# Loads re-placed, head gates from a 0/1 table, swapped K halves and a last store from ScalarE, in a fused attention and feed-forward kernel

## The chip, the cores and the metric

The kernel runs on one core of one Trainium2 chip. The metric is device time in microseconds (us) of one execution; lower is better. The engines are named PE (TensorE, with its weight loads as PEld), DVE (VectorE), ACT (ScalarE), POOL (GpSimd) and SP (SyncE, which here only issues transfers).

## What is computed

One input x of 2048 tokens by 512 columns, bf16, goes through two branches that are mixed by a gate per token. Attention runs in four segments of 512 tokens with 32 heads of 16 columns; later segments also read a memory that the earlier ones wrote.

```python
def _A_ref(x, wq, wk, wv, wo, beta):            # H = 32, N = 4 segments, L = 512
    q, k, v = ...                               # x @ wq, x @ wk, x @ wv by head and segment
    phi = lambda t: jnp.where(t > 0, t + 1.0, jnp.exp(t))
    g = _sigmoid(beta).reshape(1, H, 1, 1)
    for s in range(N):
        logits = qs @ ks^T * scale + causal mask
        a_dot = softmax(logits) @ vs
        a_mem = (phi(qs) @ M) / (phi(qs) @ z + 1e-06)
        outs.append(g * a_mem + (1.0 - g) * a_dot)
        M = M + phi(ks)^T @ vs
        z = z + phi(ks) summed over tokens
    return concat(outs) @ wo

def _B_ref(x, W_gate, W_up, W_down):            # 512 -> 1792 -> 512
    return (relu(x @ W_gate) * (x @ W_up)) @ W_down

g = _sigmoid((x * gate_w).sum(-1, keepdims=True))
return g * _A_ref(x, ...) + (1 - g) * _B_ref(x, ...)
```

## The kernel before

All work is a list of tasks. Each task has an engine and a function that writes its instructions, and the table ORDER says in which order the tasks are written out. Each engine works through its own instructions in that order, and waits on semaphores for what other engines and transfers have to deliver. A second table, UNITS, says which PSUM bank or ring buffer each result takes.

**Segments and units.** The work on a segment is cut into four units of eight heads. A unit has four scores (`qk`, L626), each 8 matmuls on 32 rows into four PSUM banks, followed by one exponential on ACT (L648) into a buffer E. A mask on POOL (L677) sets what lies above the diagonal to zero. Every second unit has a fifth score for the diagonal blocks (`qk_diag`, L639, with L659 as its mask on DVE). The product with V (`pv`, L699) is two sets of 32 matmuls on 32 columns each, one for even heads (r = 0) and one for odd heads (r = 1); it reads V from `Vp`, and for the diagonal blocks from `Vm`, a copy by `fill_vm` (L612) that has the first half of each key block twice.

**Between the scores.** The projections, the feed-forward matmuls and the output matmuls fill PE's time between the scores. They are written by `full` either as one matmul on the whole array (L469) or as four on a quarter of the columns each (L473), whichever fits the tile shape in use.

**K.** `proj_k` casts k from PSUM into `ktr` (L575) and then multiplies it by 0/1 columns (L578): `mcol_e` keeps the rows of even heads, `mcol_o` those of odd heads. A key block is 128 keys, held as two halves of 64. `KT` has five halves for each block: two of even heads, one extra first half of even heads, and two of odd heads. The diagonal score reads the two that stand in the middle, first halves of even and of odd heads. That makes three products for each unit.

**Head gates.** `head_gates` works on 32 gates (L386 to L388). `row_gates` then copies, for each quarter of the partitions, the gates that this quarter needs (L393, L395, five copies for each of four quarters), and `pair_gates` finishes (L399).

**Loads.** All loads are issued at the start, on SP's queue, but for three on ACT's (L266): half of the first x quarter (`xn`), wq row block 1, and wq row blocks 2 and 3 in one transfer. The second half of the first segment's x comes transposed by the transfer (`xT`, L304); the first half is transposed by PE. The weights of the down projection (`wd`) and of the output projection (`wo`, L325 and L327) are the last of these loads. On SP's queue everything later, such as transposes of `pkT` (L591), the next segment's x (L276), the coefficients (L773, L787) and the output stores (L900), comes behind them.

**The end.** The last output tile is computed in columns 0 to 255, then 256 to 383 and 384 to 511. DVE scales each part by the token's gate (L895), and SP issues two stores (L900).

Of the kernel before, what the change touches and what calls it, by code (L numbers as in the profile page):

```python
# [12 lines left out]
P = 128  # L13
# [165 lines left out]
def kernel(  # L179
# [74 lines left out]
    def work():  # L254
        return plan.one("ps", range(7, -1, -1))


    LANDS = dict(n0=3470, n1=3600, q0=4650, q1=4650, x0=6300, qb=6000, ka=7900, kb=9300,
                 v=11500, g0=13000, u0=14000, gw=14800, be=15100, g1=16300, u1=17500, n2=18500,
                 x1=21500, g2=22800, u2=23900, g3=25000, u3=26100, d0=28900, d1=31600, o=34400)  # L260

    def arrival(name):
# [717 lines left out]
```

## Time and profile before

| | |
|---|---|
| three runs | 264.25 us (median), 263.18 to 264.29 |
| the profiled execution | 264.48 us, of which its span is 262.7 |
| PE busy | 257.8 us, 98% of the span |
| DVE, ACT, POOL busy | 204.9 us (78%), 183.7 us (70%), 64.2 us (24%) |
| granted TensorE clock | 1.0 |
| transfers | 19.72 MB, mean 75 GB/s |

Matmuls are pipelined and their ends are modelled, so a busy PE is not PE at its peak. The other engines count only for what PE has to wait for. In rows of the timeline the columns are start, length, engine, line, operation, result and operands, count, and in square brackets the idle time in front with what ended it. In rows of groups they are busy time and mean duration in ns of one, then the idle time in front of them. In tables by stage the columns are the stretch, its length, busy time and count for each engine, granted clock, share of the DMA engines, and GB/s.

### The profile page before, as it was taken

What the parts mean: (1) busy time and instruction counts of PE and PEld (TensorE: products, weight loads), DVE (VectorE), ACT (ScalarE), POOL (GpSimd) and SP (SyncE); (2) the same over time, 40 slices, a digit from 0 to 9 for tenths busy, and PEclk for the clock granted to TensorE, in tenths of its full rate; (3) what the DMA queues carried; (4) which work ended last, traced back from release to release, by engine and by line L of the source; (5) the groups of instructions that cost most, each with busy time, mean ns of one, the idle gap of its engine ahead of it and who ended that gap; (6) DMA issues with size and microseconds to landing.
All of it is one profiled execution on the core that took longest, in us unless ns stands there. A gap on an engine that the chain in (4) does not pass through costs nothing.

```text
span 262.7 us, 8841 instructions
## 1 busy us (share of the span) xinstructions
PE 257.8 (98%) x3828; PEld 117.4 (45%) x3828; DVE 204.9 (78%) x472; ACT 183.7 (70%) x168; POOL 64.2 (24%) x168
## 2 busy tenths in 40 slices
PE   8899999999999999999999999999999999999995
PEld 3344434454444454444444445444444444444454
DVE  2798999999995756959989789676998858688722
ACT  3199889999788678888486776878568759873000
POOL 8022732212321423232031223133121243121000
PEclk9999999999999999999999999999999999999999
DMA  6999984110711201200220111320110200311011
GB/s 146 337 304 323 273 192 53 22 24 10 116 25 52 92 22 39 76 2 2 80 41 4 56 20 36 110 85 2 24 57 3 56 2 22 102 30 73 2 42 42
DMA packets 31566, 19.72 MB, mean 75 GB/s; under 512 B 16040, under 2 KB 29992, under 8 KB 31528
## 3 DMA queue, kind: packets, MB, share of 16 engines
q1 hardware_dynamic: 30840, 18.64, 26.2%
q8 instruction: 30, 0.49, 0.9%
q10 hardware_dynamic: 688, 0.52, 0.9%
q14 instruction: 8, 0.07, 0.1%
HBM read 13.21 MB, written 2.55 MB: 60 GB/s over the span
## 4 chain that ended last, share of the span: by engine, by line
PE 94%; DMA 2%; DVE 2%; SPq 0%; issue 0%
PE ps L469 56%; PE ps L473 20%; PE ps L626 8%; PE ps L699 7%; DMA xT<-in_A_x_dram 2%; PE ps L639 1%; DVE QT L559 1%; PE ps L819 1%; PE ps L795 0%; PE ps L755 0%; SPq L266 0%; DVE KT L578 0%; DVE ktr L575 0%; DVE osr L895 0%
## 5 line engine op out<-in xcount | busy, mean ns | idle before, releaser
L648 ACT ACTIVATE E<-ps 128x2048 bf16<-128x2048 f32 x64 | 120.2, 1877 | 27.3 <-PE ps L626 18.8
L677 POOL TENSOR_SCALAR_AFFINE_SELECT E<-E 128x256 bf16<-128x256 bf16 x128 | 54.8, 452 | 169.8 <-ACT E L648 169.8
L869 DVE TENSOR_TENSOR hT<-ps,rgr 128x512 bf16<-128x512 f32 x56 | 38.0, 684 | 17.0 <-PE ps L469 12.6
L469 PE MATMUL ps<-xT,wu_sb 128*128 128x512 bf16 x168 | 45.9, 380 | 0.0
L469 PE MATMUL ps<-xT,wg_sb 128*128 128x512 bf16 x154 | 42.0, 380 | 0.0
L863 ACT ACTIVATE rgr<-ps 128x512 bf16<-128x512 f32 x56 | 32.5, 599 | 13.4 <-PE ps L473 6.9
L469 PE MATMUL ps<-wd_sb,hT 128*128 128x512 bf16 (+1 forms) x174 | 40.3, 354 | 0.0
L730 DVE STREAM_TRANSPOSE T<-ps 128x512 f32<-128x512 f32 x32 | 22.2, 707 | 7.8 <-PE ps L699 7.7
L626 PE MATMUL ps<-QT,KT 32*128 32x320 bf16 (+3 forms) x512 | 25.4, 273 | 0.1
L469 PEld LDWEIGHTS <-wu_sb 128*128 128x128 bf16 x168 | 15.1, 98 | 18.7 <-issue 2.7
L469 PEld LDWEIGHTS <-hT 128*128 128x128 bf16 x174 | 15.2, 98 | 17.1 <-issue 2.1
L469 PEld LDWEIGHTS <-wg_sb 128*128 128x128 bf16 x154 | 14.4, 98 | 17.7 <-issue 1.3
L895 DVE TENSOR_SCALAR osr<-ps,ngcol 128x512 bf16<-128x512 f32 (+2 forms) x18 | 12.2, 685 | 11.2 <-PE ps L473 5.7
L699 PE MATMUL ps<-E,Vp 128*17 128x320 bf16 (+3 forms) x512 | 19.3, 274 | 0.0
L626 PEld LDWEIGHTS <-KT 32*128 32x128 bf16 x512 | 7.6, 92 | 25.5 <-issue 24.2
L473 PE MATMUL ps<-xT,wg_sb 128*32 128x512 bf16 x280 | 18.6, 379 | 0.0
L648 ACT ACTIVATE Em<-ps 128x2048 bf16<-128x2048 f32 x8 | 15.0, 1876 | 5.0 <-PE ps L639 5.0
L473 PE MATMUL ps<-wd_sb,hT 128*32 128x512 bf16 (+1 forms) x312 | 17.8, 360 | 0.0
L469 PE MATMUL ps<-xT,wq_sb 128*128 128x512 bf16 x60 | 16.4, 382 | 1.0 <-DMA xT<-in_A_x_dram 1.0
L469 PE MATMUL ps<-wv_sb,xT 128*128 128x512 bf16 x62 | 16.9, 380 | 0.0
L559 DVE CAST QT<-ps 128x512 bf16<-128x512 f32 x16 | 10.7, 687 | 6.4 <-PE ps L469 6.2
L473 PE MATMUL ps<-xT,wu_sb 128*32 128x512 bf16 x224 | 15.1, 379 | 0.0
(102 smaller groups left out, 301.3 us busy)
## 6 DMA issues: line engine op xcount, KB each, us to landing
out_dram<-osr SPq DMA_DIRECT2D x15, 128.0 KB
wd_sb<-in_B_W_down_dram SPq DMA_DIRECT2D x2, 896.0 KB
xn<-in_A_x_dram SPq DMA_DIRECT2D x3, 512.0 KB
cdr<-coefs SPq DMA_DIRECT2D x6, 256.0 KB
xn<-coefs SPq DMA_DIRECT2D x6, 256.0 KB
wg_sb<-in_B_W_gate_dram SPq DMA_DIRECT2D x2, 512.0 KB
wu_sb<-in_B_W_up_dram SPq DMA_DIRECT2D x2, 512.0 KB
wg_sb<-in_B_W_gate_dram SPq DMA_DIRECT2D x2, 384.0 KB
```

The lines of the kernel that those rows point to most:

```text
L469: nc.tensor.matmul(out, lhsT=lhsT, rhs=rhs, start=start, stop=stop)
L473: nc.tensor.matmul(out[r], lhsT=lhsT[:, r], rhs=rhs, start=start, stop=stop, tile_position=(0, 32 * j))
L559: prj["q", seg, c] = plan.add("DVE", 600, key - RQK, lambda: nc.vector.tensor_copy(QT[i][:], bank(sl)), [a], DVL, frees=[sl])
L626: nc.tensor.matmul(ps[:, j * L + o:j * L + o + L - q], lhsT=KT[i][rows, kb, 3 * r:3 * r + 2].rearrange("p h q -> p (h q)"), rhs=QT[i][rows ...
L639: nc.tensor.matmul(ps[:, o:o + HP], lhsT=KT[i][rows, kb, 2:4].rearrange("p h q -> p (h q)"), rhs=QT[i][rows, kb * P:kb * P + HP], start=Tr ...
L648: last_exp[0] = [plan.add("ACT", 66 + 4 * L / 1.2, key, lambda: nc.scalar.activation(dst, ps[:, 0:4 * L], ACT.Exp, scale=SCALE), [a] + war ...
L677: nc.gpsimd.affine_select(out=m[:, :, o:o + HP], in_=m[:, :, o:o + HP], compare_op=ALU.is_ge, fill=0.0, base=HP, pattern=[[0, 4], [1, HP]] ...
L699: nc.tensor.matmul(bank(sl)[32 * m:32 * m + HW, q:q + w], lhsT=(Vp[i] if n < 4 else Vm)[:, kb, r, 4 * c + j, 0:HW], rhs=rhs, start=(n == 0 ...
L730: done.append(plan.add("DVE", 633, key - RL, lambda r=r, sl=sl: nc.vector.transpose(T[ts.i][:, r], bank(sl)), [a] + done, 75 if r else 0, ...
L863: r = plan.add("ACT", 478, key - RL, lambda sl=gsl, rs=rs: nc.scalar.activation(rgr[rs.i][:], bank(sl), ACT.Relu), [g], ACL, frees=[gsl])
L869: nc.vector.tensor_tensor(hT[hs1.i][:], bank(sl), rgr[rs.i][:], ALU.mult)),
L895: nc.vector.tensor_scalar(osr[os.i][:, n0 - c0:n1 - c0], bank(sl)[:, 0:n1 - n0], ngcol[:, tt:tt + 1], None, ALU.mult)),
```

## The change

1. **Loads.** wq row blocks 2 and 3 become two transfers on SP's queue, issued behind the transposing load of x, in place of one on ACT's. The q matmuls of the first segment wait for each row block. `wd` and `wo` become tasks of their own (`load_late`) that ORDER places later on SP's queue, among the first segment's transfers.
2. **Head gates.** POOL fills a 0/1 table `pick` by memsets. DVE multiplies it with beta and sums over four columns, which leaves in each partition the betas it needs; then one exponential and five small DVE operations follow.
3. **K halves.** `KT` has four halves: even heads second half first, then odd heads in the usual order. The middle two are again the first halves, so the third product is gone. Since the even heads' keys are swapped within each block, so must be V: `Vs` is a copy of the even heads' V with halves swapped, made by two transfers for each segment on SP's queue. `pv` for even heads waits for it. POOL masks only half of the partitions for even heads.
4. **The end.** ACT scales the last 128 columns, and ACT's queue issues the last store.
5. **Order.** ORDER and UNITS are replaced whole (not shown). Among other things six v matmuls now stand ahead of the first score.

```diff
+    Vs = sb([P, 4, H // 2, 18], BF16, "Vs")
-    KT = [sb([P, 4, 5, P // 2], BF16, f"KT{i}") for i in range(RQ)]
+    KT = [sb([P, 4, 4, P // 2], BF16, f"KT{i}") for i in range(RQ)]
...
-    got_q = [load(eng, wq_sb[:, ci, :], A_wq[ci * P:(ci + 1) * P, :], "q%d" % ci)
-             for ci, eng in enumerate((nc.sync, nc.scalar))]
+    def load_wq(eng, ci):
+        return load(eng, wq_sb[:, ci, :], A_wq[ci * P:(ci + 1) * P, :], "q%d" % ci)
+    got_q = [load_wq(nc.sync, 0), load_wq(nc.scalar, 1)]
     nc.sync.dma_start_transpose(out=xT[0][:, NC // 2:NC, :], in_=x[0:L, halves[1]])
-    got_q.append(load_rows(nc.scalar, wq_sb, A_wq, 1, "q"))
+    got_q += [load_wq(nc.sync, ci) for ci in range(2, NC)]
...
-    got_d = [load_wd(0, 7, "d0"), load_wd(7, NF, "d1")]
-    (seven wo transfers at the start)
+    def load_late():
+        for j, (f0, f1) in enumerate(((0, 7), (7, NF))):
+            got_d.append(plan.add("SP", 1270, K(2 + j), lambda f0=f0, f1=f1: nc.sync.dma_start(
+                out=wd_sb[:, f0:f1, :], ...
+        for c in range(NC):
+            ...
+            got_o.append(plan.add("SP", 1250 if c else 600, K(4, c), wo, lat=3500, xfer=450.0))
...
+    nc.gpsimd.memset(pick[:], 0.0)
+    for m in range(4):
+        rows = slice(32 * m, 32 * m + 32)
+        nc.gpsimd.memset(pick[rows, 1, :, m], 1.0)
+        for c in range(NC):
+            nc.gpsimd.memset(pick[rows, 0, c, (m + c) % 4], 1.0)
+    def pick_heads():
+        nc.vector.tensor_tensor(gsel..., pick..., betab[:, None, :].to_broadcast([P, 2, H]), ALU.mult)
+        nc.vector.tensor_reduce(out=gcat..., in_=gsel..., axis=mybir.AxisListType.X, op=ALU.add)
...
-                KT[u % RQ][:, :, o:o + w],
-                ktr[ks.i].rearrange("p (k h q) -> p k h q", k=4, h=2)[:, :, 0:w], m[:, 0:1],
+                KT[u % RQ][:, :, 2 * n:2 * n + 2],
+                ktr[ks.i].rearrange("p (k h q) -> p k h q", k=4, h=2)[:, :, ::1 if n else -1],
+                m[:, 0:1],
...
+        att["vs", seg] = [plan.add("SP", 600, K(4 * seg - 2 - (1 if seg else 0), 2000), lambda h=h: (
+            nc.sync.dma_start(out=Vs[64 - 64 * h:128 - 64 * h], in_=Vp[i][64 * h:64 * h + 64, :, 0])),
+            ... for h in range(2)]
...
+                half = slice(0, P) if r else slice(0, HP)
                 for _, _, o in PIECES[k]:
-                    nc.gpsimd.affine_select(out=m[:, :, o:o + HP], in_=m[:, :, o:o + HP],
+                    nc.gpsimd.affine_select(out=m[half, :, o:o + HP], in_=m[half, :, o:o + HP],
...
-                            lhsT=(Vp[i] if n < 4 else Vm)[:, kb, r, 4 * c + j, 0:HW],
+                            lhsT=(Vm[:, kb, r] if n > 3 else Vp[i][:, kb, 1] if r else
+                                  Vs[:, kb])[:, 4 * c + j, 0:HW],
...
+            last = w == P and n1 == D
+                if last:
+                    nc.scalar.activation(dst, src, ACT.Copy, scale=g)
+                else:
+                    nc.vector.tensor_scalar(dst, src, g, None, ALU.mult)
+        queue = nc.scalar if last else nc.sync
```

More of the change, by code (lines that the diff above doesn't have):

```diff
@@ L390, in row_gates @@
-    def row_gates(m):
-        g = gall.rearrange("p k (c j r) -> p k c j r", j=4, r=2)
-        rows = slice(32 * m, 32 * m + 32)
-        nc.vector.tensor_copy(gcat[rows, 1], g[rows, 1, :, m])
-        for c in range(NC):
-            nc.vector.tensor_copy(gcat[rows, 0, c], g[rows, 0, c, (m + c) % 4])
-    def pair_gates():
-        for r, m in enumerate((mcol_e, mcol_o)):
-            nc.vector.tensor_scalar(bdg[:, :, r], gcat[:, 1, :, r], m[:, 0:1], None, ALU.mult)
-    got_eb = plan.add("ACT", 200, 0.0, lambda: nc.scalar.activation(
-        eb[:], betab[:], ACT.Exp, scale=-1.0), [got_be], 100)
@@ L403 @@
-    got_gates = plan.add("DVE", 700, 0.0, head_gates, [got_eb], 100, lock=True)
-    got_gates = [plan.add("DVE", 560, 0.0, lambda m=m: row_gates(m), [got_gates], 100, lock=True)
-                 for m in range(4)]
-    got_gates = plan.add("DVE", 300, 0.0, pair_gates, got_gates, 100, lock=True)
+    def pick_heads():
+        nc.vector.tensor_tensor(
+            gsel.rearrange("p k c j r -> p k (c j r)"), pick.rearrange("p k c j r -> p k (c j r)"),
+            betab[:, None, :].to_broadcast([P, 2, H]), ALU.mult)
+        nc.vector.tensor_reduce(out=gcat.rearrange("p k c r -> p (k c) r"),
+                                in_=gsel.rearrange("p k c j r -> p (k c) r j"),
+                                axis=mybir.AxisListType.X, op=ALU.add)
@@ new lines, in head_gates @@
+    def head_gates():
+        nc.vector.tensor_scalar(rcat[:], gcat[:], 1.0, None, ALU.add)
+        nc.vector.reciprocal(rcat[:], rcat[:])
+        nc.vector.tensor_tensor(gcat[:, 0], gcat[:, 0], rcat[:, 0], ALU.mult)
+        for r, m in enumerate((mcol_e, mcol_o)):
+            nc.vector.tensor_scalar(bdg[:, :, r], rcat[:, 1, :, r], m[:, 0:1], None, ALU.mult)
+    got_gates = plan.add("DVE", 380, 0.0, pick_heads, [got_be], 100, lock=True)
+    got_gates = plan.add("ACT", 200, 0.0, lambda: nc.scalar.activation(
+        gcat[:], gcat[:], ACT.Exp, scale=-1.0), [got_gates], 100)
@@ L408 @@
+    got_gates = plan.add("DVE", 850, 0.0, head_gates, [got_gates], 100, lock=True)
     PEL, DVL, ACL, POL = 230, 150, 165, 130
@@ L552, in proj_q @@
                     prev=a, start=not ci, stop=False)
-            a = matmuls(K(-4, c), [got_q[2]] + got_x[0][1], sl, proj_mm(wq_sb, c, 0)[2:], prev=a,
-                        start=False)
+            for ci in range(2, NC):
+                a = matmuls(K(-6 + ci, c), [got_q[ci]] + got_x[0][1], sl,
+                            [proj_mm(wq_sb, c, 0)[ci]], prev=a, start=False, stop=ci == NC - 1)
         else:
@@ L638, in qk_diag @@
                     o = j * L + 4 * HP * v + HP * kb
-                    nc.tensor.matmul(ps[:, o:o + HP], lhsT=KT[i][rows, kb, 2:4].rearrange(
+                    nc.tensor.matmul(ps[:, o:o + HP], lhsT=KT[i][rows, kb, 1:3].rearrange(
                                          "p h q -> p (h q)"),
```

75 lines of the change are left out of this document (37 added, 38 removed), and 124 rows, old and new, of the table ORDER.

## The prediction

> **What bounds the kernel now.** I read the page first, for the engine that is never free, then the chain of waits, for where that engine is not yet running or already done.
>
> ```profile
> span 262.7 us, 8841 instructions
> PE 257.8 (98%) x3828; PEld 117.4 (45%) x3828; DVE 204.9 (78%) x472; ACT 183.7 (70%) x168; POOL 64.2 (24%) x168
> 7.73 0.61 PE ps L469 x2
> 8.36 2.48 DVE QT L559 x4
> 10.84 0.61 DVE ktr L575
> 11.48 0.82 DVE KT L578 x3
> 12.34 0.40 PE ps L626 x8
> 12.74 2.70 PE ps L469 x12
> 15.44 0.33 PE ps L626 x8
> ...
> 30.91 1.22 PE ps L699 x64
> 32.13 1.29 PE ps L473 x24
> ...
> 257.66 2.13 PE ps L469 x36
> 259.82 0.35 DVE osr L895
> PE ps L469 <- DMA xT<-in_A_x_dram: 1.0, 1, 1.0
> 12.34:259.79 247.45, 247.43 (x3784) 112.96 (x3784) 199.28 (x454) 181.03 (x164) 58.76 (x144) 1.00 0.25 68
> ```
>
> The first two lines are the page's. The lines after them are pieces of the chain (start, length, what). The second to last is from the list of PE's waits, the last from the table by stages: between 12.34 and 259.79 PE is busy 247.43 of 247.45 us, at a granted clock of 1.00. So the kernel has three parts: 12.34 us up to the first score, 247.45 us in which TensorE does not stop, and 2.9 us (262.7 less 259.8) behind its last matmul. The only wait longer than 0.9 us in PE's list is for the first transposed half of x.
>
> What PE has to do does not change. In the built instruction lists both kernels have 152 runs of one tile shape, and the same columns: 672 whole 512-column matmuls become 676, and 952 quarter ones become 936 (sixteen quarters are four whole ones). A run of 12 whole ones stays 2.70 us, a score 0.33, a PV pair 1.22 with 1.29 of filling. Nothing can be won in the 247 us, only lost. The gain has to come from the two ends.
>
> **The start.** PE's rows there, the data rate by stages, and four groups by shape:
>
> ```profile
> 4.75 2.01 PE L469 MATMUL ps<-xT,wq_sb 128*128 128x512 bf16 x8
> 7.73 1.89 PE L469 MATMUL ps<-xT,wq_sb 128*128 128x512 bf16 x8 [0.97 <-DMA xT<-in_A_x_dram]
> 9.45 2.75 PE L469 MATMUL ps<-xT,wk_sb 128*128 128x512 bf16 x12
> 3.65 0.80 PEld L506 LDWEIGHTS <-xn 128*128 128x128 bf16 x8 [0.57 <-DMA xn<-in_A_x_dram]
> 0.00:3.00 3.00, 2.16 (x6) 0.79 (x7) 0.51 (x7) 0.65 (x1) 2.15 (x10) 1.00 0.24 72
> 0.00:4.00 4.00, 3.16 (x11) 1.12 (x12) 0.51 (x7) 1.28 (x1) 3.15 (x10) 1.00 0.45 135
> 4.00:7.00 3.00, 2.76 (x16) 1.47 (x15) 0.85 (x2) 0.74 (x2) 2.33 (x15) 1.00 1.10 183
> 20.00:30.00 10.00, 10.00 (x90) 4.21 (x89) 8.89 (x28) 9.39 (x11) 4.39 (x14) 1.00 1.07 339
> L575 DVE CAST ktr<-ps 128x512 bf16<-128x512 f32 x16 | 10.8, 686 | 1.5 <-PE ps L469 1.4
> L578 DVE TENSOR_SCALAR KT<-ktr,mcol_e 128x512 bf16<-128x512 bf16 x16 | 5.4, 348 | 0.0
> L578 DVE TENSOR_SCALAR KT<-ktr,mcol_e 128x256 bf16<-128x256 bf16 x16 | 4.8, 298 | 0.0
> L395 DVE COPY gcat<-gall 32x2 f32<-32x2 f32 x16 | 1.9, 182 | 0.0
> ```
>
> In the rows by stage the last number is GB/s. From 7.73 PE runs 8 q matmuls and 12 k matmuls until 12.20 (9.45 + 2.75): 4.47 us for 20, 0.2235 each. In the changed order six v matmuls stand ahead of the first score: 26 matmuls, 5.81 us. With S the start of the second q group, the first score comes at S + 5.81, with six matmuls (1.34 us) already done that before came behind it. The gain is therefore 12.34 + 1.34 - 5.81 - S = 7.87 - S: 0.14 us even if S stays at 7.73, because the v matmuls fill the gap before the first score.
>
> DVE does not hold that score back. Its chain was QT 2.48, ktr 0.61, KT 0.82; now it is QT, two ktr casts (0.61 + 0.69) and one KT product (0.35), since the first score needs only the even product. That is 4.13 from S + 0.63, so S + 4.8, a microsecond inside S + 5.81. Should the swapped halves cost the product its speed, up to a cast's 0.69, it is still inside.
>
> S itself is the landing of the last of three: the transposed half of x and wq rows 2 and 3, which move from ACT's queue to SP's, behind the transpose. I take what one queue holds to land in its order; then 1.05 MB (two xn quarters, wq 0 and 1, the transposed half at 0.26 MB, wq 2 and 3) have to come through. The rows give 0.54 MB in the first 4 us and 0.55 MB in the next 3, so 1.05 MB at 6.8 us. How long after its last byte a load can be used: the two xn quarters (0.26 MB) are through at 3.15 us by 72 and 135 GB/s, and PE starts on them at 3.65, 0.5 later. So S = 7.3 and the gain 0.57 us. Bounds: S cannot help below 6.76, where the first q group ends (4.75 + 2.01), a gain of 1.11. At worst the transpose lands when it does now and the 0.26 MB of wq follow at 339 GB/s, 0.76 later: S = 8.45, a loss of 0.58. I take 0.57, because the byte count is the nearest row.
>
> Here the Trainium skill speaks to the same transfer. "DMA: Bandwidth & Descriptors", section "Queues, rings and completion order", says each DMA engine takes turns between the queues that have work, so the wq load on ACT's queue slowed the transpose; its section on latency and other measured facts gives transposes 261 GB/s, by which, as an estimate, the transpose would take 1.0 us and S would be at its lower bound. The trace disagrees so far: 183 GB/s in the stretch that holds the transpose and a plain load.
>
> **The stretch behind it.** Every score needs the exponential of the one before to have ended.
>
> ```profile
> 18.85 1.88 ACT L648 ACTIVATE E<-ps 128x2048 bf16<-128x2048 f32 x1
> 20.66 1.58 ACT L863 ACTIVATE rgr<-ps 128x512 bf16<-128x512 f32 x3
> 22.11 1.90 ACT L648 ACTIVATE E<-ps 128x2048 bf16<-128x2048 f32 x1
> 19.50 1.88 SPq L266 DMA_DIRECT2D wu_sb<-in_B_W_up_dram  x1
> 24.02 0.08 DVE L423 DVE_READ_ACCUMULATOR junk<-xn,gwb 128x1 f32 x1
> 32.57 1.26 SPq L591 DMA_TRANSPOSE pK<-pkT  x1
> SPq L787 <- DMA coefs<-dnr: 9.6, 4, 4.0
> ```
>
> From start to start E takes 1.81 and a short ACT operation 0.48 (1.45 for three). Up to the first PV the changed order alternates 12 and 10 whole matmuls between scores, periods of 3.03 and 2.58; ACT has E and two short operations in each, 2.78. Over two periods that is 5.61 on PE against 5.56 on ACT: even, with the first exponential's cover of 0.7 in hand (it starts 0.40 behind its score and takes 1.88; the next score comes after 3.03). I cost this at nothing.
>
> The Vs copies are new and the first PV waits for them. They stand on SP's queue behind the loads up to wu (issued at 21.4: 19.50 + 1.88), a pK transpose (1.26) and the second xn load, which waits for the last gate product on DVE. That ended at 24.1; ahead of it now go the head gates, three groups of row copies and three third products, 3.6 us without the head gates (three groups of five copies of 0.18, three products of 0.30), so 20.5. Then SP is at 22.7, xn and two Vs issues of about 0.6 bring it to 24.5, and a small transfer lands 4.0 us after issue at the longest wait shown: 28.5. The first PV comes at 30.91 - 0.57 = 30.3. The cover is 1.8 us. At the three later segment ends PE has, counted in runs of the new order at the durations above, over 10 us of other work between the last PV that reads the old Vs and the first that needs the new one, and what queues on SP behind that wait (output stores, coefficient loads) is not waited for sooner. wd and wo come later on the queue, but the first of their readers is past 60 us.
>
> Sixteen third products (4.8 us) and the row copies leave DVE, which is not the bound: zero. POOL's masks on half the partitions and its 21 small memsets: zero, POOL is 24% busy.
>
> **The end.**
>
> ```profile
> L521 ACT CAST xT<-ps 128x256 bf16<-128x256 f32 x2 | 0.7, 372 | 0.7 <-PE ps L506 0.7
> L863 ACT ACTIVATE rgr<-ps 128x512 bf16<-128x512 f32 x56 | 32.5, 599 | 13.4 <-PE ps L473 6.9 <-PE ps L469 5.4 <-ACT rgr L863 0.8
> 0.80 0.48 ACTq L266 DMA_DIRECT2D xn<-in_A_x_dram  x1
> L900 SPq DMA_DIRECT2D out_dram<-osr x17: 332/337/458, 78.7 to 260.2; - x17
> ```
>
> ACT at 256 and 512 columns costs 0.372 and 0.599, so 0.26 at 128 against DVE's 0.35: 0.09 gained. A DMA issue on ACT took 0.48 against 0.34 on SP: 0.14 lost. I take 0, between +0.15 and -0.15.
>
> **Sum.** 0.57 + 0 + 0. The profiled execution took 264.48 us, of which 1.8 lie around its span; the median of the three runs is 264.25 (263.18 to 264.29), so the two agree within 0.1%. The forecast is 264.25 - 0.57 = 263.7 us. About 0.5% (1.32 us) is what a measurement of this kernel can tell from no change, so I call it no change.
>
> **The rivals.**
>
> - The whole wait for x goes. S is 6.76, the gain 1.11, with 0.15 at the end 1.26: 263.0. For it: without the wq load beside it the transpose has the engines to itself. Against it: wq 3 still has to come last. The 261 GB/s of the Trainium skill's "DMA: Bandwidth & Descriptors" would lead here too.
> - ACT falls behind, and the kernel is slower. Place: the scores from 13 to 60 us, 17 in the chain of before. If the two short operations of a period cost their whole 0.60 instead of 0.48, each period is 0.24 longer on ACT. It decides once ACT is later than its cover of 0.7. Price: 6 x 0.24 - 0.7 = 0.7 when only the stretch up to the first PV is hit, 17 x 0.24 - 0.7 = 3.4 when all is; the middle, 2.1, less 0.57 gives +1.5: 265.8. For it: ACT is busy 9.39 of the 10 us from 20 to 30. Against it: before ran the same operations at 0.48.
> - The re-placed loads do not do what they should: wq 3 lands behind a transpose that is no faster, S is 8.45, +0.58: 264.8.
>
> **How the numbers follow.** Forecast 0.42, whole wait gone 0.30, ACT behind 0.18, loads later 0.10. The 0.5% line on the fast side is 262.93; the first rival stands 0.1 from it, and runs of before scatter by 1.1 us, so I put two thirds of it beyond: 0.20 faster. The slow line is 265.57: 0.16 of ACT behind and 0.02 of the loads, 0.18 slower. The rest, 0.62, is no change. The range goes from 262.6 (first rival less 0.4 of scatter) to 265.9 (the ACT rival's middle); left out are half of that rival and a few hundredths below.
>
> **What would show it.** Right: the second q group starts at about 7.3 instead of 7.73, the first score comes near 13.1, the first PV near 30.3, PE is busy without a gap from then to about 259.2, and the end behind it stays 2.9 us. The forecast is wrong if PE's list of waits names exponentials, Vs or a weight load for over a microsecond in all, if the second q group starts below 6.9 or above 7.8, or if the end behind the last matmul differs from 2.9 by more than 0.3.

## The result and the profile after

| | kernel before | changed kernel |
|---|---|---|
| median | 263.85 us (263.18 to 264.59, 22 runs) | 264.25 us (263.23 to 265.37, 22 runs) |
| profiled execution, and its span | 264.48 us, 262.7 us | 264.98 us, 261.9 us |

The ratio is 1.0020, with a 95% interval of 1.0011 to 1.0029: in this comparison the changed kernel is slower by 0.3 to 0.8 us. The forecast was 263.7 us, a gain of 0.57. The time is inside the forecast's range, but the sign is wrong. That 263.7 comes near at all is in part luck: it was worked out from a median of 264.25 over three runs, and 22 runs of before have 263.85.

The two profiles alone would have said that the forecast holds. These are PE's rows at the start of the changed kernel, one row of its weight loads, the first product with V, and the end (PE's last rows, the last scale on ACT and the last store's issue).

```profile
span 261.9 us, 8799 instructions
PE 255.2 (97%) x3787; PEld 118.0 (45%) x3816; DVE 199.8 (76%) x437; ACT 184.1 (70%) x169; POOL 62.9 (24%) x189
4.56 4.00 PE L480 MATMUL ps<-xT,wq_sb 128*128 128x512 bf16 x15
8.40 0.59 PE L480 MATMUL ps<-xT,wk_sb 128*128 128x512 bf16 x2
8.83 0.38 PE L480 MATMUL ps<-xT,wq_sb 128*128 128x512 bf16 x1
9.04 2.32 PE L480 MATMUL ps<-xT,wk_sb 128*128 128x512 bf16 x10
11.45 1.25 PE L480 MATMUL ps<-wv_sb,xT 128*128 128x512 bf16 x5
12.86 0.40 PE L642 MATMUL ps<-QT,KT 32*128 32x448 bf16 x8
11.45 0.98 PEld L480 LDWEIGHTS <-xT 128*128 128x128 bf16 x6 [0.58 <-DMA wv_sb<-in_A_wv_dram]
30.10 0.61 PE L716 MATMUL ps<-E,Vs 128*17 128x448 bf16 x16
258.64 0.39 PE L480 MATMUL ps<-wo_sb,oT 128*128 128x128 bf16 x4
259.06 0.37 ACT L917 ACTIVATE osr<-ps,ngcol 128x128 bf16<-128x128 f32 x1 [15.55 <-PE ps L480]
259.46 0.35 ACTq L925 DMA_DIRECT2D out_dram<-osr  x1
```

The q matmuls run without the wait of 0.97 us that the profile of before has, and the span is 0.8 us shorter. (PE's busy time is lower because 29 of 3816 matmuls have no record here; the weight loads are complete.) One new thing stands in the weight loads' row: the first one of the v matmuls waited for wv. PE still had work queued and lost only 0.1 us in this execution.

Two things make the pair of profiles misleading. First, the start differs between executions of the same kernel by about as much as the change was to bring. The changed kernel's 22 spans go from 261.4 to 263.7, with a median of 262.4; in the other comparisons the median span of the kernel before was 261.8 to 262.4. Second, this execution took 264.98 us with a span of 261.9: 3.08 us lie outside the span, where before had 1.78. Both are followed up below.

### The profile page after: what moved, and what is told of

It reads as the page before. It is cut to its first block, busy times and chain, and to the rows that moved or that the text cites. A ratio compares the mean times of both kernels' runs of the same rounds, so it can differ in the third digit from the quotient of the medians.

```text
span 261.9 us, 8799 instructions
## 1 busy us (share of the span) xinstructions
PE 255.2 (97%) x3787; PEld 118.0 (45%) x3816; DVE 199.8 (76%) x437; ACT 184.1 (70%) x169; POOL 62.9 (24%) x189
## 4 chain that ended last, share of the span: by engine, by line
PE 91%; DMA 2%; SPq 2%; DVE 1%; issue 1%; ACT 1%; DVEq 0%; ACTq 0%
PE ps L480 54%; PE ps L484 20%; PE ps L642 8%; PE ps L716 7%; DMA wv_sb<-in_A_wv_dram 2%; SPq L267 1%; PE ps L655 1%; ACT E L664 1%; PE ps L837 1%; DVE T L748 1%; SPq L304 1%; PE ps L773 0%; PE ps L813 0%; DVE osr L919 0%; ACT rgr L881 0%
## 5 line engine op out<-in xcount | busy, mean ns | idle before, releaser
L694 POOL TENSOR_SCALAR_AFFINE_SELECT E<-E 128x256 bf16<-128x256 bf16 (+1 forms) x128 | 52.8, 435 | 169.4 <-ACT E L664 169.3
L480 PE MATMUL ps<-xT,wg_sb 128*128 128x512 bf16 x162 | 44.8, 380 | 0.4 <-issue 0.2
L480 PE MATMUL ps<-xT,wu_sb 128*128 128x512 bf16 x150 | 41.8, 380 | 0.6 <-issue 0.5
L480 PE MATMUL ps<-wd_sb,hT 128*128 128x512 bf16 (+1 forms) x157 | 37.1, 351 | 0.6 <-issue 0.5
L480 PEld LDWEIGHTS <-wg_sb 128*128 128x128 bf16 x170 | 15.8, 98 | 19.7 <-issue 1.9
L480 PEld LDWEIGHTS <-hT 128*128 128x128 bf16 x164 | 14.0, 98 | 16.2 <-issue 3.4
L484 PE MATMUL ps<-wd_sb,hT 128*32 128x512 bf16 (+1 forms) x352 | 20.7, 362 | 0.0
L484 PE MATMUL ps<-xT,wu_sb 128*32 128x512 bf16 x264 | 17.6, 379 | 0.0
L480 PE MATMUL ps<-xT,wk_sb 128*128 128x512 bf16 x57 | 15.8, 380 | 0.4 <-issue 0.2
L484 PE MATMUL ps<-xT,wg_sb 128*32 128x512 bf16 x216 | 14.5, 379 | 0.0
```

The lines of the kernel that those rows point to most:

```text
L480: nc.tensor.matmul(out, lhsT=lhsT, rhs=rhs, start=start, stop=stop)
L484: nc.tensor.matmul(out[r], lhsT=lhsT[:, r], rhs=rhs, start=start, stop=stop, tile_position=(0, 32 * j))
L694: nc.gpsimd.affine_select(out=m[half, :, o:o + HP], in_=m[half, :, o:o + HP], compare_op=ALU.is_ge, fill=0.0, base=HP if r else 0, pattern ...
```

## The experiments

Three theories were put against each other. **A**: up to some 17 us PE is fed by one stream of loads, and a wait that is taken away at x comes back at wv or at the load behind it. **B**: wv is late only because its issue was moved back on SP's queue, so another place would cure it. **C**: the time goes elsewhere (the swap of V's halves, the new end, ACT, or outside the span). A fourth, **D**, came up on the way, for the time outside the span.

All kernels were timed in five rounds beside the kernel before on the same chip. The median of before was 263.99 us beside e1 to e4, 264.05 beside e5 to e8 and e13 to e16, 263.55 beside e9 to e12, and 264.12 beside e17 and e18; a ratio is not the quotient of two medians, as e3 shows. "Waits" are those of PE in the one profiled execution.

| run | median us | ratio to before (95%) | median span | waits at the start, us |
|---|---|---|---|---|
| e1 before again | 263.93 | 1.0002 (0.9989 to 1.0015) | 262.2 | none |
| e2 after again | 264.07 | 1.0006 (0.9992 to 1.0019) | 262.15 | wq 0.26, wv 0.69, wg 0.16 |
| e3 after, old end | 263.91 | 1.0013 (0.9997 to 1.0029) | 262.15 | wv 1.37 |
| e4 after, wq rows on ACT | 264.06 | 1.0000 (0.9986 to 1.0014) | 262.2 | x 0.98 |
| e5 before, wq rows on SP | 264.34 | 1.0006 (0.9995 to 1.0017) | 262.6 | wk 0.28 |
| e6 after, score first | 264.63 | 1.0023 (1.0010 to 1.0036) | 262.7 | KT 0.78 |
| e7 after, wv on ACT | 266.84 | 1.0106 (1.0077 to 1.0135) | 265.05 | wq 2.27 |
| e8 after, wq rows split | 264.00 | 1.0004 (0.9994 to 1.0014) | 262.05 | none |
| e9 after, wv in halves | 264.14 | 1.0025 (1.0009 to 1.0041) | 262.25 | wg 0.28 |
| e10 after, finer warming | 264.44 | 1.0029 (1.0016 to 1.0042) | 262.7 | wq 0.19, wg 0.34 |
| e11 before, wq rows split | 263.85 | 1.0005 (0.9994 to 1.0015) | 262.15 | wq 0.54 |
| e12 after, split and halves | 263.92 | 1.0011 (0.9998 to 1.0025) | 262.1 | wq 0.84 |
| e13 after, no wv load | 263.59 | 0.9983 (0.9970 to 0.9997) | 261.75 | wq 0.23 and 0.16 |
| e14 before, no wv load | 264.03 | 0.9996 (0.9982 to 1.0011) | 262.3 | x 0.31, cast of xT 0.16 |
| e15 after, split, finer warming | 263.83 | 0.9994 (0.9982 to 1.0007) | 262.1 | wk 0.58 |
| e16 after, no V copies | 264.23 | 1.0007 (0.9992 to 1.0022) | 262.45 | wv 1.05 |
| e17 after, wk columns, finer warming | 264.42 | 1.0016 (1.0005 to 1.0026) | 262.7 | wk 0.39, wv 0.55, wg 0.52 |
| e18 as e17, wq rows split | 263.78 | 0.9988 (0.9976 to 1.0000) | 262.0 | none |

**Where in the program the executions differ.** The start of the first product with V, in the first and second profile of before, the second of the changed kernel, and e16:

```profile
30.84 0.61 PE L699 MATMUL ps<-E,Vp 128*17 128x448 bf16 x16
30.28 0.61 PE L699 MATMUL ps<-E,Vp 128*17 128x448 bf16 x16
30.96 0.61 PE L716 MATMUL ps<-E,Vs 128*17 128x448 bf16 x16
31.32 0.62 PE L716 MATMUL ps<-E,Vp 128*17 128x448 bf16 x16
```

From there to the end of the span it is 231.8 to 232.15 us in all twenty profiles, of either kernel and of every edit (before 262.7 less 30.84, the changed kernel 261.9 less 30.10). So within the span, differences of more than some 0.3 us arise up to this point, and theory C has little room behind it. With an unchanged start the product comes at 30.84 and 30.28 us in before (mean 30.6) and at 30.10, 30.96, 30.96 and 31.32 in the changed kernel, e2, e3 and e16 (mean 30.8). That is the sign of the result, but the scatter is larger than the difference.

**e1 and e2: the two kernels once more, unchanged.** What was expected:

> The kernel before, unchanged, for a second profile and its spans. Theory 1 (one profile is one draw of the start): the wait for the transposed x is not 0.97 us again but differs by some tenths, and the spans scatter around 262.1 (median time 263.85 less some 1.75), half a microsecond under the 262.7 of the first profile. Theory 2 (the new end costs) and theory 3 (new waits in the middle) say nothing on it. Ratio 1.000.

> The changed kernel, unchanged, for a second profile. Ratio 1.002. Theory 1: the start again gives PE its second q group at once (first score near 12.9), and the difference in spans to the kernel before is some 0.3 us the slow way, so that the 0.7 us won before the first score is lost behind it or was not won on average. Theory 3: this profile shows waits of PE on ACT or DVE of 0.5 to 1 us between the first score and 259 us, which the first profile did not.

PE's rows of before (first fence) and of the changed kernel (second), second profiles:

```profile
4.66 4.39 PE L469 MATMUL ps<-xT,wq_sb 128*128 128x512 bf16 x16
8.89 2.75 PE L469 MATMUL ps<-xT,wk_sb 128*128 128x512 bf16 x12
11.78 0.40 PE L626 MATMUL ps<-QT,KT 32*128 32x448 bf16 x8
```

```profile
4.67 3.64 PE L480 MATMUL ps<-xT,wq_sb 128*128 128x512 bf16 x15 [0.26 <-DMA wq_sb<-in_A_wq_dram]
11.81 1.25 PE L480 MATMUL ps<-wv_sb,xT 128*128 128x512 bf16 x5 [0.69 <-DMA wv_sb<-in_A_wv_dram]
13.21 0.40 PE L642 MATMUL ps<-QT,KT 32*128 32x448 bf16 x8
```

The wait for x, the one thing that the forecast wanted to win, isn't there in this execution of before: 16 q matmuls in one run, and the first score comes at 11.78 instead of 12.34. In the changed kernel wv is waited for. e2's ratio, 1.0006 (0.9992 to 1.0019), agrees with the 1.0020 of the first comparison and also with no change: that the gain is gone is shown twice, a loss of 0.3 us or more only once. The rows also hold the reason why x was in time in e1: at 0.2235 us each the k matmuls would start 3.58 us behind the first q matmul, not 4.23 (8.89 less 4.66). Some of the first matmuls took twice as long. The weight loads of the same execution show it by their distance, 0.43 and then, within the last row, 0.22 (2.26 us for eleven):

```profile
5.06 0.15 PEld L469 LDWEIGHTS <-wq_sb 128*128 128x128 bf16 x1 [0.28 <-issue]
5.49 0.15 PEld L469 LDWEIGHTS <-wq_sb 128*128 128x128 bf16 x1 [0.28 <-issue]
5.92 0.15 PEld L469 LDWEIGHTS <-wq_sb 128*128 128x128 bf16 x1 [0.28 <-issue]
6.30 2.26 PEld L469 LDWEIGHTS <-wq_sb 128*128 128x128 bf16 x11 [0.23 <-issue]
```

So three things share the start and cover one another: the landing of x, the landing of what comes after it, and none (e2, e3, e4) to five (e8, e18) q matmuls at half speed, which cost 0.2 us each. The granted clock reads 1.00 over this stretch all the while. The Trainium skill, "TensorE: Matmul & The Clock Gate", section "What's actually happening", says that PE starts at half rate and that a window which runs freely against the kernel decides when it rises; the rows agree: in e2 all q matmuls from 4.67 us on are at full speed, in e1 those from 6.3 on.

**e3 and e4: the changed kernel with one part undone.** e3 has the old end, e4 has wq rows 2 and 3 on ACT's queue again.

```diff
-            last = w == P and n1 == D          # e3
+            last = False
...
-    got_q += [load_wq(nc.sync, ci) for ci in range(2, NC)]     # e4
+    nc.scalar.dma_start(out=wq_sb[:, 2:4, :], in_=A_wq.rearrange(...)[:, 2:4, :])
```

> The changed kernel with the last 128 columns scaled by VectorE and stored by SyncE as before. Theory 2: the time falls by 0.4 us or more, to a ratio of 1.000 or below. Theories 1 and 3: no change, 1.002.

> The changed kernel with wq row blocks 2 and 3 loaded in one transfer on ScalarE's queue as before. If the order of these loads is what removed the wait for x, the wait is back, near 1 us, less what the six v matmuls ahead of the first score absorb: slower by 0.5 to 1.0 us than the changed kernel, ratio 1.004 to 1.006. If that wait was a draw, no change: 1.002.

Two rows of e3 and two of e4:

```profile
12.30 1.25 PE L480 MATMUL ps<-wv_sb,xT 128*128 128x512 bf16 x5 [1.37 <-DMA wv_sb<-in_A_wv_dram]
13.70 0.40 PE L642 MATMUL ps<-QT,KT 32*128 32x448 bf16 x8
```

```profile
7.43 1.67 PE L482 MATMUL ps<-xT,wq_sb 128*128 128x512 bf16 x7 [0.98 <-DMA xT<-in_A_x_dram]
13.14 0.40 PE L644 MATMUL ps<-QT,KT 32*128 32x448 bf16 x8
```

The old end changes nothing that can be measured. With the wq rows back on ACT's queue the wait for x is back (0.98) and the wait for wv is gone: the two are exchanged by this one load. With everything else of the change in place the time is that of before, 1.0000, and not 1.004 to 1.006 as expected: the wait came back, and the time did not rise with it. So the rest of the change is worth nothing within 0.4 us, as forecast. The data rates say how the exchange comes about. These are the stages 4 to 7 and 7.5 to 10.5 us of before, of the changed kernel and of e4, in this order; the last two numbers are the share of the DMA engines and GB/s:

```profile
4.00:7.00 3.00, 2.76 (x16) 1.47 (x15) 0.85 (x2) 0.74 (x2) 2.33 (x15) 1.00 1.10 183
7.50:10.50 3.00, 2.77 (x13) 1.27 (x13) 2.14 (x4) 0.00 (x0) 0.00 (x0) 1.00 1.10 348
```

```profile
4.00:7.00 3.00, 3.00 (x15) 1.47 (x14) 0.78 (x2) 0.75 (x2) 2.70 (x23) 1.00 1.06 280
7.50:10.50 3.00, 3.00 (x15) 1.37 (x14) 2.48 (x4) 0.00 (x0) 0.21 (x5) 1.00 0.87 236
```

```profile
4.00:7.00 3.00, 2.32 (x15) 1.01 (x13) 0.74 (x2) 0.65 (x2) 2.70 (x23) 1.00 1.13 206
7.50:10.50 3.00, 3.00 (x15) 1.35 (x15) 2.44 (x4) 0.00 (x0) 0.19 (x5) 1.00 1.10 350
```

With all of wq's second half behind the transpose on one queue, the first stage is faster (280 GB/s) and the second slower (236). What x gains, wk and wv lose. The second stage is the steadier sign: 236 to 301 GB/s in the profiles of the changed kernel, e2, e3, e5, e6, e9, e10, e16 and e17, which have both wq rows on SP's queue, and 346 to 350 in before, e1, e4 and e14. The first stage scatters: 239 to 283 in the former, 183 to 285 in the latter. Why the rate sags is open.

**e5 and e11: the loads alone, on the kernel before**, with its order, in which the first score stands ahead of the v matmuls. e5 puts both wq rows on SP's queue, e11 row 2 on SP's and row 3 on ACT's.

```diff
-    got_q.append(load_rows(nc.scalar, wq_sb, A_wq, 1, "q"))
+    for ci, eng in ((2, nc.sync), (3, nc.sync)):       # e5;  e11: (3, nc.scalar)
+        eng.dma_start(out=wq_sb[:, ci, :], in_=A_wq[ci * P:(ci + 1) * P, :])
+    got_q.append(arrival("qb"))
```

> The kernel before with one edit: rows 2 and 3 of wq are two loads on SP's queue behind the transposing load of x, as in the kernel after; PE's order stays that of before, with the first score ahead of the v matmuls. Theory A (the start's loads are one stream through the DMA engines: x earlier makes wv later, and PE waits for one or the other): no wait for x, second q group at 6.3 to 6.8 us; wv lands at 11.4 to 12.3, after the first score at 11.3 to 11.8, so PE waits 0 to 0.9 us for wv behind the first score; span 261.3 to 262.3, ratio 0.998 to 1.000. Theory B (wv is late because it was put a us later in SP's queue): the same here. Theory C (the slowdown of the changed kernel has nothing to do with these loads): no run with over 2.2 us outside the span, and the time that of before; if it belongs to the loads, one run in five here has 2.2 to 3.1 us outside the span, as in the changed kernel.

> The kernel before with one edit: row 2 of wq on SP's queue behind the transposing load of x, row 3 on ScalarE's. Theory A: x waits no more than 0.3 us, wv's issue moves by 0.5 only and its v matmuls stand behind the first score, so nothing waits for it; first score 11.4 to 11.8 (half-speed matmuls remain), span 261.6 to 262.1, ratio 0.998 to 0.9995. Theory B (any wq row on SP's queue costs as much as it brings): ratio 1.0000 to 1.001.

In e5 x is in time and wk is not; in e11 wq itself is waited for. Neither is faster than before: with the order of before, too, the wait for x goes and the time stays.

**e6, e7, e8, e9, e12: other orders and queues for the changed kernel.**

```diff
-    62 112 63 77 65 122 113 108 ...       # e6, ORDER: score 122 ahead of v matmuls 106, 107, 112
+    74 64 62 63 122 106 107 112 77 65 113 108 ...
...
-    got_v = load_cols(nc.sync, wv_sb, A_wv, 0, D, "v")       # e7
+    got_v = load_cols(nc.scalar, wv_sb, A_wv, 0, D, "v")
...
+    got_q += [load_wq(eng, ci) for ci, eng in ((2, nc.sync), (3, nc.scalar))]     # e8, e12
...
+    for i in range(2):                                       # e9, e12; ORDER: 112 ahead of 107
+        nc.sync.dma_start(out=wv_sb[:, 2 * i:2 * i + 2, :], in_=A_wv...[:, 2 * i:2 * i + 2, :])
```

> The changed kernel with the first score put ahead of the six v matmuls in PE's order (and of nothing else). Theories A and B: first score at 11.2 to 11.8 us instead of 12.9 to 13.7; the wait for wv stays, smaller by the score's 0.33 us: 0.2 to 1.0; span 0.3 below the changed kernel's, ratio to the kernel before 0.9985 to 1.0005. If the wait for wv is not what costs the time (theory C): the span stays as it was within 0.1.

> The changed kernel with wv's load issued on ScalarE's queue, right behind row 1 of wq (at 1.9 us instead of 5.3). Theory A (one stream): the wait for wv goes, and a wait of 0.5 to 1.4 us for x, wq or wk comes in its place; span as the changed kernel's within 0.3, ratio 0.999 to 1.003. Theory B (SP's queue order): no wait for wv and none of over 0.2 us for x, wq and wk; first score at 12.2 to 12.5, span 0.6 to 1.3 below the changed kernel's, ratio 0.996 to 0.998.

> The changed kernel with row 3 of wq on ScalarE's queue and row 2 on SP's. Theory A: x waits 0 to 0.5 us, wv 0 to 0.7, in sum as in the changed kernel; first score 12.8 to 13.4. Theory B: wv is issued at 4.8 instead of 5.3 us, its wait is less by 0.45 and x still needs no wait: first score 12.4, span 0.45 below the changed kernel's, ratio 0.998.

> The changed kernel with wv loaded by two DMAs of two rows of blocks each, in the same place of SP's queue, and two groups of v matmuls exchanged, so that four of the six need the first half only. Theory A (PE's start is bound in turn by x's landing, wv's landing, and the half-speed first matmuls): four matmuls (0.9 us) run before the second half is needed, so the wait for wv goes from 0.6 to 1.4 us down to 0 to 0.5; first score 12.2 to 13.2, span 0.3 to 0.7 below the changed kernel's, ratio 0.998 to 1.000. Theory C (what the changed kernel loses is not there): ratio 1.0005 to 1.002 as before.

> The changed kernel with both: row 3 of wq on ScalarE's queue, and wv by two DMAs with the v groups exchanged. Theory A: no wait over 0.2 us for x or wv in any execution, so that only the half-speed matmuls set the first score: 12.2 to 13.1 us; span 0.3 to 0.6 below the kernel before's, ratio 0.9975 to 0.9995. Theory C: as the changed kernel, 1.000 to 1.002.

One row of e6, one of e7, and two of e9:

```profile
12.05 0.40 PE L642 MATMUL ps<-QT,KT 32*128 32x448 bf16 x8 [0.78 <-DVE KT L590]
```

```profile
9.41 3.17 PE L480 MATMUL ps<-xT,wq_sb 128*128 128x512 bf16 x7 [2.27 <-DMA wq_sb<-in_A_wq_dram]
```

```profile
11.24 1.24 PE L483 MATMUL ps<-wv_sb,xT 128*128 128x512 bf16 x5
16.87 0.60 PE L483 MATMUL ps<-xT,wg_sb 128*128 128x512 bf16 x2 [0.28 <-DMA wg_sb<-in_B_W_gate_dram]
```

e7 speaks against B: at this place wv comes in time, and wq is late by 2.27 us, more than either wait before and more than A's 0.5 to 1.4. After that idle stretch the q matmuls are at half speed again (3.17 us for seven in the row), and here the granted clock shows it, 0.51 in the stage from 9.4 to 12.8 us:

```profile
9.40:12.80 3.40, 3.39 (x9) 1.23 (x10) 1.57 (x3) 0.00 (x0) 0.00 (x0) 0.51 1.10 348
```

Eight matmuls at 0.43 instead of 0.22 add about 1.7 us to the price. e6 missed its expectation of 11.2 to 11.8: the score needs DVE's KT first, at 12.05, and the kernel is slower, not 0.3 faster. e9 shows how a wait moves on. The wait for wv is gone, the first score comes at 12.63 instead of 12.86, and its span is 0.3 longer, not shorter, than that of the changed kernel's profile: with both executions set side by side at their last weight load, e9 is 0.50 us ahead of the changed kernel's profile in front of the second piece of wg and 0.04 ahead behind it. e2 (0.56, then 0.23) and e10 (0.58, then 0.08) lose in the same place. But e9's ratio, 1.0025, is not the 0.998 to 1.000 that A had promised for it, and e12's 1.0011 is not 0.9975 to 0.9995: A as written for these runs ended at wv, and had to be widened to the load behind it. e8 has no wait at all, and there the half-speed matmuls fill the time.

**e13 and e14: what wv's load costs.** Both kernels without it; the v matmuls read wk.

```diff
-    got_v = load_cols(nc.sync, wv_sb, A_wv, 0, D, "v")
+    got_v = arrival("v")
-            lambda ci=ci: (xT[seg % 3][:, ci, t * P:(t + 1) * P], wv_sb[:, ci, :])
+            lambda ci=ci: (xT[seg % 3][:, ci, t * P:(t + 1) * P], wk_sb[:, ci, :])
```

> The changed kernel with the load of wv left out; the v matmuls read wk's columns instead, so V is computed with wk (that part of the result is another). Theory A (PE's start is fed by one stream of loads, and a wait taken away at x comes back at wv and then at the next load): without wv's 0.5 MB no wait of over 0.2 us is left between 4 and 20 us, first score 11.7 to 12.4 us, span 260.8 to 261.5, ratio 0.995 to 0.998. Theory C (the time is lost elsewhere): ratio 0.9995 to 1.002, as with wv.

> The same edit on the kernel before (V computed with wk, no load of wv). Theory A: x stands ahead of wv in the queue, so its wait of 0 to 1 us stays, and nothing else waited: first score 11.8 to 12.4, span 261.6 to 262.5, ratio 0.998 to 1.001; the changed kernel without wv is then the faster one by 0.3 to 0.9 us, which is what the forecast had promised for it with wv. If wv's load slows x's too: ratio under 0.998.

PE at the v matmuls and the first score in e13, and at the second q group and first score in e14:

```profile
11.22 1.24 PE L480 MATMUL ps<-wk_sb,xT 128*128 128x512 bf16 x5
12.61 0.40 PE L642 MATMUL ps<-QT,KT 32*128 32x448 bf16 x8
```

```profile
6.54 1.89 PE L469 MATMUL ps<-xT,wq_sb 128*128 128x512 bf16 x8 [0.31 <-DMA xT<-in_A_x_dram]
11.16 0.40 PE L626 MATMUL ps<-QT,KT 32*128 32x448 bf16 x8
```

Without 0.5 MB of wv in the stream the kernel before gains nothing (0.9996) and the changed one gains what the forecast had promised it: 0.9983, with a median span of 261.75 against 262.3 for before on the same chip, 0.55 us. That is the sharpest evidence for A: the gain at x exists, and wv and what follows it take it back. (The intervals of e13 and e14 overlap, so the difference between these two is not beyond doubt; those of e13 and of the first comparison do not.) It was less than expected here as well (a first score at 12.61, not 11.7 to 12.4), since waits of 0.2 for wq remain.

**e16: no V copies.** The two transfers of each segment are left out, and the even heads read V unswapped.

```diff
-            nc.sync.dma_start(out=Vs[64 - 64 * h:128 - 64 * h], in_=Vp[i][64 * h:64 * h + 64, :, 0])),
+            None),
...
-                            lhsT=(Vm[:, kb, r] if n > 3 else Vp[i][:, kb, 1] if r else
-                                  Vs[:, kb])[:, 4 * c + j, 0:HW],
+                            lhsT=(Vm if n > 3 else Vp[i])[:, kb, r, 4 * c + j, 0:HW],
```

> The changed kernel without the copies that swap the halves of V for the even heads (eight transfers less on SP's queue; the even heads then multiply swapped keys with unswapped values, so that part of the result is another). The forecast put them at nothing: ratio to the kernel before as the changed kernel's, 1.000 to 1.003, the first P times V at the same distance from the first score (17.3 us). If they cost something: that distance shrinks and the ratio falls to 0.999 or below.

1.0007, against 1.0006 in e2 and 1.0020 in the first comparison: no cost that a time of this scatter could show. The profiles show a small one. These are V's last cast and the issue of the copies in the changed kernel, and the weight loads of the first product with V in e17:

```profile
23.72 0.58 ACT L617 CAST Vp<-ps 128x512 bf16<-128x512 f32 x1
24.38 1.38 SPq L628 DMA_DIRECT2D Vs<-Vp  x2
33.17 0.36 PEld L721 LDWEIGHTS <-Vs 128*17 128x17 bf16 x16 [1.77 <-DMA Vs<-Vp]
```

The copies' issues end at 25.8 us, not at the forecast's 24.5: they start when V's last cast on ACT has ended, at 24.30, which the forecast did not count. In thirteen profiles, e16 among them, the product starts 0.32 or 0.33 us behind the score ahead of it. In the changed kernel, e2, e3, e9, e10 and e15 it is 0.37 to 0.54, and in e17 1.91. Only in e17 does the profile name the copies, so for the others it is likely and not shown. The cover of 1.8 us that the forecast gave the copies was about nothing.

**e10 and e15: the time outside the span.** In 19 of 135 runs of kernels with the changed order of work, 2.1 to 3.1 us lie outside the span; in 204 runs of before and of kernels made from it, never more than 1.9. In the changed kernel's profile, the stretch behind the span (262.2 to 266 us, span 261.9) holds a single packet, a block of instructions:

```profile
DMA packets 1, 0.02 MB, mean 4 GB/s; under 512 B 0, under 2 KB 0, under 8 KB 0
q8 instruction: 1, 0.02, 1.8%
```

e3's profile has the same, before's has no packet there. Theory D is that this fetch past the program's end holds up the end. The test is to make PE's program 36 instructions longer with the same columns (e15 adds e8's split):

```diff
-        for k in range(7):
-            w = L if k < 6 else P
+        for k in range(25):
+            w = P
```

> The changed kernel with the warming matmuls cut finer: 25 of 128 columns instead of 6 of 512 and one of 128, the same columns in all, 36 PE instructions more. Two profiles of the changed kernel's PE program show a last block of instructions (16 KB) fetched after the last instruction, and 10 of its 58 runs (with the old end or old wq place among them) have 2.1 to 3.1 us outside the span, none of 111 of the kernel before's. Theory D (a fetch past the program's end, set by where the PE program's end falls in a block, holds up the end): none of the runs here is over 2.1 us outside the span, and the last fetch comes ahead of the end; span as the changed kernel's within 0.2. Without D: 2 or 3 of 12 runs are over 2.1.

> The changed kernel with row 3 of wq on ScalarE's queue and the warming matmuls cut finer (25 of 128 columns, 36 PE instructions more). Theory D (an instruction block fetched past the program's end holds up the end in some runs): no run over 2.1 us outside the span, against 4 of 12 with the wq rows split alone; median 263.5 to 264.0, ratio 0.998 to 1.000. Without D: 2 to 4 of 12 over 2.1.

Of the 58 runs that the expectation speaks of, 9 and not 10 are over 2.1 us. With the longer program (e10, e15, e17, e18) none of 49 runs is over 2.1 us; at 19 in 135 seven would be expected. That supports D, but does not show it: e3's profile has the late packet and only 2.01 us outside its span, and e8 had four such runs out of 12 with its last block fetched ahead of the end in the profile. How a fetch would do it stays open. It is worth 0.2 us in the mean of the changed kernel's 22 runs and nothing in their median (1.75 us outside the span, as before). e10's spans show that it isn't the main cause: 262.7.

**e17 and e18: less ahead of wv.** The last 128 columns of wk (128 KB) are loaded behind wv, with the finer warming; e18 also splits the wq rows as e8 does.

```diff
+    for i in range(2):
+        nc.sync.dma_start(out=wk_sb[:, 2 * i:2 * i + 2, 0:3 * P], in_=wk[:, 2 * i:2 * i + 2, 0:3 * P])
+    nc.sync.dma_start(out=wv_sb[:], ...)
+    nc.sync.dma_start(out=wk_sb[:, :, 3 * P:D], in_=wk[:, :, 3 * P:D])
```

> The changed kernel with 128 KB less ahead of wv: the last 128 columns of wk, which PE needs much later, are loaded behind wv; and the warming matmuls cut finer (25 of 128 columns). Theory A: wv lands 0.3 to 0.5 us earlier (128 KB at 250 to 350 GB/s), its wait shrinks by as much, 0 to 0.9 us is left; span 0.2 to 0.5 below the changed kernel's, ratio 0.9985 to 1.0005. Theory D: no run over 2.1 us outside the span. If the stream's slow stretch only moves with the loads: as the changed kernel, 1.0005 to 1.002.

> The same with row 3 of wq on ScalarE's queue as well. Theory A: no wait for wv, 0 to 0.6 us for x, wq or wk; span 261.6 to 262.1, ratio 0.9975 to 0.9995, faster than both kernels. Otherwise 0.9995 to 1.001, as with the split rows and the finer warming matmuls alone.

A row from e17's profile, of its first product with V, and two from e18's:

```profile
33.20 0.62 PE L721 MATMUL ps<-E,Vs 128*17 128x448 bf16 x16 [1.51 <-POOL rq L455]
```

```profile
4.57 4.48 PE L485 MATMUL ps<-xT,wq_sb 128*128 128x512 bf16 x15
13.08 0.40 PE L647 MATMUL ps<-QT,KT 32*128 32x448 bf16 x8
```

e17 gained nothing; the waits of its profile are wk, wv, wu and wg in turn. That profile is its slowest run (266.68 us) and waits 1.51 us more at the first product with V. The row names POOL, but the weight loads of the same product name the copies Vs (1.77, shown under e16). e18 is the fastest kernel that computes everything: 263.78 us, 0.9988 (0.9976 to 1.0000), 0.3 us under before, with no wait for a load left and five half-speed matmuls instead. Its interval reaches 1.0000, so it is faster than before only just.

In sum, A is borne out as a mechanism: in every profile with no wait for x, another load's wait or half-speed matmuls stand in its place. As a number it was too kind. The ratios that it led to expect did not come in e5, e6, e7, e9, e11, e12, e17 and, by little, e13, each time on the slow side.

## Why the prediction was wrong

- **The step that failed is the start.** The forecast put six v matmuls between the k matmuls and the first score ("26 matmuls, 5.81 us") and asked when x and wq land, but not when wv does, though those six need it and its issue moves from 4.31 to 5.29 us on SP's queue. In six profiles with both wq rows on SP's queue (after, e2, e3, e10, e16, e17) PE waited 0.1, 0.7, 1.4, 0, 1.05 and 0.55 us for wv, 0.6 in the mean: the size of the gain that was forecast. The loads behind wv were put at nothing as well, and wg was waited for in e2, e9, e10 and e17 (0.16 to 0.52).
- **S was right as a mechanism and pessimistic in size.** In the changed kernel nothing waits for x; the second q group starts at 6.9 (eight matmuls from 4.56, three at half speed). That is the first rival's condition, "the whole wait for x goes", to which 0.30 was given; its time of 263.0 didn't come, for the same reason. In e2, e3 and e10 the second q group starts earlier still, at 6.3 to 6.5 (eight times 0.2235 behind the first q matmul).
- **The wait of 0.97 was read from one execution as if every run had it.** The sentence that the profiled time and the median "agree within 0.1%" was true and proved nothing about the start: e1 had no wait for x, and its first score came 0.56 earlier. Over the two profiles of before, the wait that could be won is 0.5 in the mean.
- **What lies behind the first score held in the first pair of profiles.** From first score to last scale before takes 247.48 us (12.34 to 259.82) and the changed kernel 246.20 (12.86 to 259.06): 1.28 less, where six v matmuls less are 1.34. ACT kept up: the first product with V came 17.24 us behind the first score, forecast 17.2. But in e2, e9 and e10 that distance is 17.7 to 17.9, with the wait for wg and a late first product with V in it. The dropped products and row copies cost and brought nothing that can be measured, and e4 confirms the sum at 1.0000 within 0.4 us. The Vs copies were mis-sized: their cover was about nothing instead of 1.8 us.
- **DVE's chain** was short by 0.3 to 0.6 us: in e6, where nothing else holds the score, S + 4.8 would be 11.4 to 11.8 (the second group starts at 6.6 and goes on at 7.0), and KT was there at 12.05. Of this, 0.54 is a wait of the casts for the k matmuls, which the chain left out. In the changed kernel the v matmuls cover that.
- **A slip in the bounds:** 7.73 and 0.76 make 8.49, not 8.45; the loss there would be 0.62 and the third rival's time 264.9 instead of 264.8. Nothing else hangs on it.
- **The end is the forecast's zero**, though both terms were off: the scale on ACT took 0.37 (0.26 was estimated), the store's issue 0.35 (0.48). From the last matmul to the end of the span it is 2.87 us (261.9 less 259.03), 2.9 before.
- **Its own signs of failure.** "A weight load for over a microsecond in all" in PE's waits is what e3 (1.37) and e16 (1.05) show for wv, and e2, e3 and e10 have the second q group below 6.9. The first profile of the changed kernel, with 0.1 and 6.9, showed none of the signs.
- **The rivals.** None of them took place as written; the first had its condition but not its time. "Loads later" had the right subject, a load that comes late because of the new queue, but the wrong load. ACT didn't fall behind.
- **The skill's rule.** The sentence from "DMA: Bandwidth & Descriptors", "Queues, rings and completion order", on engines that take turns between queues agrees with part of the profiles: in the stage 4 to 7 us before and e4 have 183 and 206 GB/s with wq beside the transpose, the changed kernel 280 without. But e1 and e14 have 234 and 285 with wq beside it, so it is not settled here. What it would make of the time stopped there: the next stage gave back what this one gained.

## What to carry to other kernels

When a step is moved ahead of another, list every load that it reads and ask when each lands; a wait that ends at a load in a stream that is full usually moves to the next load of the stream. Before a wait of under a microsecond at the start is forecast away, look at it in a second execution of the same kernel, for the start scatters by as much. To price a load, leave it out: that said more in one comparison than the other places of the loads. And compare profiles at a point that every version passes, such as the first product with V here: it says at once in which part of the program the difference arises.

## What the runs showed of the hardware

- The same loads move at 346 to 350 GB/s from 7.5 to 10.5 us when the transfer of wq rows 2 and 3 went by ACT's queue beside the transpose (before, e1, e4), and at 236 to 301 when it went by SP's behind it (changed kernel, e2, e3, e10). The bytes through at 11 us, summed from the trace's rates by half microseconds, are 2.43 and 2.64 MB in the two profiles of before, 2.46 and 2.63 in those of the changed kernel.
- The number of half-speed q matmuls at the start differs between executions from none to five, 0 to 1.0 us, and hides waits for loads; the granted clock in the page is 1.0 all the while. An idle stretch of 2.27 us (e7) brings half speed back, and there the granted clock is 0.51.
- A block of instructions can be fetched behind a program's last instruction. The Trainium skill, "Runtime: NRT & Kernel Launch", section "Instruction fetch mechanics", has the blocks of 16 KB and calls their cost mostly hidden. Here the fetch is seen in the profiles of the changed kernel and e3; 0.4 to 1.3 us more than usual at the end came in one run of seven of such kernels, and in none of 49 with 36 more PE instructions. That the one causes the other is not shown.
